# The first batch's attention values loaded in rows of 8 tokens, cast on GpSimd, spread into the key tiles by on-chip DMA, and the output product split in two

## The chip, the cores and the metric

One core of a Trainium2 chip. The metric is the device time of one execution in microseconds (us), median of several; a run is called fast or slow by its state, and ratios use fast runs only. Times inside the kernel are read from profiles of single executions, counted from the start of the span.

## The reference, cut to what matters

```python
# q, k, v: (4 batches, 8 heads, 768 tokens, 64); block = 32, window = 16
k_sum = k.reshape(B, H, 24, 32, D).max(axis=3)
v_sum = v.reshape(B, H, 24, 32, D).mean(axis=3)          # the "means"
scores_l = scale * q @ k^T, kept where |i - j| < 16
scores_s = scale * q @ k_sum^T + log(32)
a = softmax(concat(scores_l, scores_s))
attn = a @ concat(v, v_sum)
x = attn.transpose(0, 2, 1, 3).reshape(3072, 512)
out = ((sigmoid(x @ w_gate)) * (x @ w_val)) @ w_out       # 512 -> 1536 -> 512
```

## The kernel before: the parts that matter

The 768 queries of a batch are cut into 12 query tiles of 64. A query tile needs the 96 tokens around it and the 24 block summaries, so its keys and values are a tile of KX = 96 + 24 = 120 rows. P holds the exponentials of the scores, transposed: 120 rows by 64 queries. The value tile `vx[:, t]` has 96 rows of tokens and 24 rows of means, with ones in column 64 to give the sum of each row. The 24 means are the same for all 12 tiles.

```python
def load_v(b, t0, t1):                       # GpSimd's DMA queue, f32 -> bf16 on the way
    for t in range(t0, t1):
        lo, hi = max(0, QT * t - 16), min(S, QT * t + 80)
        r0 = lo - (QT * t - 16)
        nc.gpsimd.dma_start(out=vx_t[b % 2][r0:r0 + hi - lo, t, :, 0:64],
                            in_=v[b, :, lo:hi, :].transpose([1, 0, 2]))

def V(self, *_):                             # means: 12 matmuls over the 96 rows
    for t in range(NQ):
        nc.tensor.matmul(out=vsp[96:128]..., lhsT=zband[:, 30 - 2 * t:62 - 2 * t],
                         rhs=vx[0:W, t, :, 0:64], start=(t == 0), stop=(t == NQ - 1))
    # ... batch 0: copies to vx[96:120, 0], VectorE spreads to tiles 1-5, a DMA to 6-11

def A(self, p, h=None):                      # output of head pair p (h: half of the queries)
    for t in range(6 * g0, 6 * g1):
        r = 64 * (t % 2)
        for i in range(2):
            nc.tensor.matmul(out=av[r:r + 64, t // 6, (t % 6) // 2, i, 0:65],
                             lhsT=P[0:KX, i, t, :], rhs=vx[0:KX, t, 2 * p + i, 0:65],
                             start=True, stop=True)
    # ... reciprocal and scaling on VectorE

# start of the kernel, batch 0, first half of the queries
for u in a0.units("T2a S1a T3a S2a S3a V A0a A1a X0a A2a X1a"):   # T transposes, S scores,
    u()                                                           # V means, A outputs, X transposes back
f0.m1(0, 0, 0, 1)                            # first feed-forward column block, in slices
a0.A(3, 0)
...                                          # then dense: 24 column blocks, one after the other
```

The weights come by GpSimd's DMA queue, two blocks of columns at a time; the keys and queries of batch 0 and 1 by the queues of SyncE and ScalarE. The profile counts the packets of all of them on the core's 16 DMA engines.

The softmax here doesn't subtract the row's maximum and nothing guards it: scores larger than these inputs give would overflow.

Of the kernel before, what the change touches and what calls it, by code (L numbers as in the profile page):

```python
# [8 lines left out]
FP32 = mybir.dt.float32  # L9
BF16 = mybir.dt.bfloat16  # L10
AX = mybir.AxisListType
ALU = mybir.AluOpType
# [4 lines left out]
def kernel(  # L17
# [10 lines left out]
    nc = tc.nc  # L28

    B, H, S, D = q.shape  # L30
    SCALE = 1.0 / float(D) ** 0.5
    QT = 64
    NQ = S // QT
    W = 96
    NS = S // 32
    KX = W + NS
    NP = H // 2
    d_model = H * D
    d_ff = moe_w_gate.shape[1]
    NF = d_ff // 128  # L40
    HALF = S // 2

    const = ctx.enter_context(tc.tile_pool(name="const", bufs=1))
# [7 lines left out]
    hT_pool = ctx.enter_context(tc.tile_pool(name="hTp", bufs=2))  # L51
# [7 lines left out]
    def ps(shape, dtype, name):  # L59
        return psum.tile(shape, dtype, name=name, tag="mm")  # L60

    def view(ap, off, dims):
        return bass.AP(ap.tensor, ap.offset + off, [list(ap.ap[0])] + [list(d) for d in dims])
# [7 lines left out]
    vx_t = [const.tile([128, NQ, H, 66], BF16, name=f"vx{i}") for i in range(2)]  # L71
    mask = const.tile([128, NQ, QT], BF16, name="mask")
    mask3 = const.tile([W, 3, QT], BF16, name="mask3")
    zband = const.tile([W, 64], BF16, name="zband")

    for t_ in kTn_t:
        nc.vector.memset(t_[:, 0:16], 0.0)
# [9 lines left out]
    def make_masks():  # L87


        nc.gpsimd.memset(mask3, 1.0)  # L90
        nc.gpsimd.affine_select(out=mask3, in_=mask3, compare_op=ALU.is_ge, fill=0.0,
                                base=-1, pattern=[[0, 3], [-1, QT]], channel_multiplier=1)
        nc.gpsimd.affine_select(out=mask3, in_=mask3, compare_op=ALU.is_ge, fill=0.0,
                                base=31, pattern=[[0, 3], [1, QT]], channel_multiplier=-1)
        nc.gpsimd.affine_select(out=mask3[:, 0], in_=mask3[:, 0], compare_op=ALU.is_ge, fill=0.0,
                                base=-16, pattern=[[0, QT]], channel_multiplier=1)
        nc.gpsimd.affine_select(out=mask3[:, 2], in_=mask3[:, 2], compare_op=ALU.is_ge, fill=0.0,
                                base=79, pattern=[[0, QT]], channel_multiplier=-1)
# [7 lines left out]
    def make_zband():  # L106

        nc.gpsimd.memset(zband, 0.0)
        nc.gpsimd.memset(zband[:, 30:32], 1.0 / 32.0)
        nc.gpsimd.affine_select(out=zband[:, 30:32], in_=zband[:, 30:32], compare_op=ALU.is_ge, fill=0.0,  # L110
                                base=-16, pattern=[[-32, 2]], channel_multiplier=1)
        nc.gpsimd.affine_select(out=zband[:, 30:32], in_=zband[:, 30:32], compare_op=ALU.is_ge, fill=0.0,
                                base=47, pattern=[[32, 2]], channel_multiplier=-1)


    def copy(eng, out, in_):
        if eng == "act":
            nc.scalar.copy(out=out, in_=in_)
        elif eng == "dve":
            nc.vector.tensor_copy(out=out, in_=in_)  # L120
        else:
            nc.gpsimd.tensor_copy(out=out, in_=in_)  # L122

    def big():
        return vm_pool.tile([128, 2048], FP32, name="vm", tag="vm")

    def small():
        return nat_pool.tile([128, NP, 6, 128], BF16, name="nat", tag="nat")

    def load_qk(tap, b, p, st, half=None, queue=None):  # L130

        n = S if half is None else HALF
        s0 = 0 if half is None else HALF * half
        T = n // 128
        (queue or nc.sync).dma_start(
            out=st.rearrange("p h t d -> p h (t d)"),
            in_=tap[b, 2 * p:2 * p + 2, s0:s0 + n, :].rearrange("h (p t) d -> p h (t d)", t=T),
        )
        return st

    def staging(T):

        raw = small().rearrange("p a c d -> p (a c d)").bitcast(FP32)
        return [view(raw, 128 * T * i, [[64 * T, 2], [64, T], [1, 64]]) for i in range(12 // T)]
# [16 lines left out]
    def load_v(b, t0, t1):  # L161
# [7 lines that stand above are left out]
    wg_bf = const.tile([128, NP, d_ff], BF16, name="wg")  # L169
    wv_bf = const.tile([128, NP, d_ff], BF16, name="wv")  # L170
    wo_bf = const.tile([128, NF, d_model], BF16, name="wo")

    def load_w(wb, wap, f0, nf):
        nc.gpsimd.dma_start(
            out=wb[:, :, 128 * f0:128 * (f0 + nf)],
            in_=wap.rearrange("(c p) f -> p c f", p=128)[:, :, 128 * f0:128 * (f0 + nf)])
# [9 lines left out]
    class Attention:  # L186
# [61 lines left out]
        def S(self, p, hf):  # L248
# [5 lines left out]
            for t6 in range(6):  # L254
# [12 lines left out]
                    .to_broadcast([128, 2, 6 * QT]),  # L267
                op=ALU.mult)

        def V(self, *_):  # L270
            vx = self.vx
            vsp = ps([128, 512], FP32, "vsp")
            for t in range(NQ):
                nc.tensor.matmul(  # L274
                    out=vsp[96:128].rearrange("p (h d) -> p h d", h=H),
                    lhsT=zband[:, 30 - 2 * t:62 - 2 * t],
                    rhs=vx[0:W, t, :, 0:64],
                    start=(t == 0), stop=(t == NQ - 1))
            src = vsp[96:120].rearrange("p (h d) -> p h d", h=H)
            if self.b == 0:  # L280
                for p in range(NP):
                    copy("dve" if p == 0 else "act", vx[96:120, 0, 2 * p:2 * p + 2, 0:64],
                         src[:, 2 * p:2 * p + 2])
                    copy("dve", vx[96:120, 1:NQ // 2, 2 * p:2 * p + 2, 0:64],
                         vx[96:120, 0:1, 2 * p:2 * p + 2, 0:64]
                         .to_broadcast([NS, NQ // 2 - 1, 2, 64]))
                t0 = NQ // 2
            else:
                nc.scalar.copy(out=vx[96:120, 0, :, 0:64], in_=src)
                t0 = 1  # L290
            self.replicate(t0)


        def L(self, g, h=None):
# [29 lines left out]
        def A(self, p, h=None):  # L324

            P, vx = self.P[p], self.vx
            g0, g1 = (0, 2) if h is None else (h, h + 1)
            G = g1 - g0
            at = psum2.tile([128, 2, 512], FP32, name="av", tag="at")
            av = at[:, :, 0:396].rearrange("p g (a i d) -> p g a i d", a=3, i=2)  # L330
            for t in range(6 * g0, 6 * g1):
                r = 64 * (t % 2)
                for i in range(2):
                    nc.tensor.matmul(  # L334
                        out=av[r:r + 64, t // 6, (t % 6) // 2, i, 0:65],
                        lhsT=P[0:KX, i, t, :],
                        rhs=vx[0:KX, t, 2 * p + i, 0:65],
                        start=True, stop=True)
            avf = at[:, g0:g1, 0:396].rearrange("p g (e d) -> p g e d", d=66)
            rec = xs_pool.tile([128, 2, 6, 1], FP32, name="rec", tag="rec")  # L340
            nc.vector.reciprocal(out=rec[:, 0:G], in_=avf[:, :, :, 64:65])  # L341
            xs = xs_pool.tile([128, 6, 2, 64], BF16, name="xs", tag="xs")
            nc.vector.tensor_tensor(  # L343
                out=xs[:, 0:3 * G].rearrange("p (g a) i d -> p g (a i) d", g=G),
                in0=avf[:, :, :, 0:64],
                in1=rec[:, 0:G].to_broadcast([128, G, 6, 64]),
                op=ALU.mult)
            self.xs[p] = xs
# [72 lines left out]
    def spread(base, extra, lo, hi):  # L421
# [9 lines left out]
        while j < m:  # L431
# [9 lines left out]
    a0 = att[0]  # L441

    raw = [big(), big()]
    sk = [load_qk(k, 0, p, view(raw[p // 2], 768 * (p % 2), [[384, 2], [64, 6], [1, 64]]))
          for p in range(NP)]
    sq = [load_qk(q, 0, p, st, half=0, queue=nc.scalar) for p, st in enumerate(staging(3))]

    def cast0(p):
        srcs[0][p] = [cast_qk(sk[p], "dve"), cast_qk(sq[p], "act")]

    load_v(0, 0, 3)
    make_masks()
    load_v(0, 3, 6)
    make_zband()
    load_v(0, 6, NQ)
    for f0, nf in ((0, 1), (1, 1), (2, 2), (4, 2), (6, 2), (8, 2), (10, 2)):
        for wb, wap in ((wg_bf, moe_w_gate), (wv_bf, moe_w_val)):
            load_w(wb, wap, f0, nf)

    cast0(0)  # L460
    cast0(1)
# [4 lines left out]
    a0.S(0, 0)  # L466
    cast0(3)
    f0 = Ffn(0, xTs[0])
    for u in a0.units("T2a S1a T3a S2a S3a V A0a A1a X0a A2a X1a"):
        u()  # L470
    f0.m1(0, 0, 0, 1)
    a0.A(3, 0)
# [4 lines left out]
    f0.m1(0, 0, 3, 4)  # L477


    for p, st in enumerate(staging(3)):  # L480
        srcs[0][p].append(cast_qk(load_qk(q, 0, p, st, half=1), "pool"))
    for i in range(6):
# [27 lines left out]
    for b in range(B):  # L510
# [7 lines left out]
        else:  # L518
            base = m1[0] + m1[1] + ffn.units2()
# [45 lines left out]
```

## Time and profile before

| | before |
|---|---|
| median time | 255.83 us (255.1 to 258.29, 3 runs) |
| span of the profiled execution | 252.9 us |
| first output product waits until | 22.03 us |
| dense feed-forward work from | 30.99 us |
| first transposes of the second half of the queries | 36.59 us |

(The view of the chain, which the prediction uses, puts the start of a matmul that follows another some 0.2 us later than the timeline does: 31.19 for this 30.99. All starts of dense work below are from the timeline.)

The rows of a timeline are: start, duration, engine, line, operation, output and inputs, shapes, count, and in brackets the idle time before it with what ended it. Two rows of the kernel before: 22 of the 24 output products of head pairs 0 and 1, and the 12 of pair 2. In the chain these twelve take 0.48 us, 0.04 us each.

```profile
22.72 0.61 PE L334 MATMUL av<-vx,P 120*64 120x65 bf16 x22 [0.45 <-DVE vx L120]
24.98 0.55 PE L334 MATMUL av<-vx,P 120*64 120x65 bf16 x12
```

### The profile page before, as it was taken

The page shows a single profiled execution, that of the slowest core. Times are in us where ns is not written, and L with a number is a line of the kernel's source. Part 1 is how long each engine was busy: PE and PEld are TensorE (multiplying, and loading weights), DVE is VectorE, ACT ScalarE, POOL GpSimd, SP SyncE. Part 2 cuts the span into 40 slices and gives each one's busy share as a digit, 9 for nine tenths or more (in the row PEclk, how much of TensorE's full clock was granted, in tenths as well). Part 3 has the DMA queues.
Part 4 walks back from the last instruction along what each step waited for, and adds up shares of the span by engine and source line. Part 5 has one row for each costly group of instructions (what it writes and reads, how often), then busy time and mean ns, then how long its engine had stood idle before and what let it go on. Part 6 is the DMA issues. An engine that isn't in the chain of part 4 may idle for free.

```text
span 252.9 us, 5010 instructions
## 1 busy us (share of the span) xinstructions
PE 232.6 (92%) x1980; PEld 129.6 (51%) x1992; DVE 122.4 (48%) x243; ACT 107.7 (43%) x193; POOL 111.1 (44%) x151
## 2 busy tenths in 40 slices
PE   1666899798999999999999999999999999999993
PEld 1433455466654455555554445555554466665441
DVE  5965237936971331976553307766543034444000
ACT  2851338356874243455551123555511143333121
POOL 8897167389999239996059970000000000000000
PEclk9999579999999999999999999999999999999999
DMA  6999999999999989799999995800024310000132
GB/s 213 241 158 178 221 270 281 268 171 124 128 120 144 212 208 208 148 155 187 194 119 156 223 170 145 126 14 3 0 72 146 116 44 0 1 3 0 49 117 83
DMA packets 100686, 34.25 MB, mean 135 GB/s; under 512 B 84496, under 2 KB 97208, under 8 KB 100280
## 3 DMA queue, kind: packets, MB, share of 16 engines
q0 software_dynamic: 70720, 12.46, 65.0%
q1 hardware_dynamic: 28856, 20.70, 32.5%
q10 hardware_dynamic: 1088, 0.79, 1.0%
q8 instruction: 15, 0.25, 0.4%
q14 instruction: 7, 0.06, 0.1%
HBM read 34.34 MB, written 6.29 MB: 161 GB/s over the span
## 4 chain that ended last, share of the span: by engine, by line
PE 85%; DVE 4%; DMA 2%; ACT 2%; issue 1%; ACTq 0%; DVEq 0%
PE gp L391 26%; PE vp L391 25%; PE m L408 23%; PE sc L257 3%; PE av L334 3%; PE vsp L274 3%; DMA vx<-vx 2%; PE br L362 2%; PE tp L197 1%; DVE vx L120 1%; DVE kTx L233 1%; ACT kTn L203 1%; DVE P L264 1%; DVE kTx L237 0%; DVE xs L343 0%
## 5 line engine op out<-in xcount | busy, mean ns | idle before, releaser
L399 DVE SCALAR_TENSOR_TENSOR hT<-gate,vp 128x384 bf16<-128x384 f32 x96 | 52.8, 551 | 68.7 <-PE vp L391 63.9
L391 PE MATMUL gp<-xT,wg 128*128 128x384 bf16 x384 | 80.6, 332 | 1.1 <-ACT xT L365 1.1
L391 PE MATMUL vp<-xT,wv 128*128 128x384 bf16 x384 | 80.1, 330 | 0.0
L398 ACT ACTIVATE gate<-gp 128x384 f32<-128x384 f32 x96 | 47.3, 493 | 53.6 <-DVE hT L399 43.7
L408 PE MATMUL m<-wo,hT 128*128 128x512 bf16 x276 | 64.3, 379 | 0.6
L391 PEld LDWEIGHTS <-wv 128*128 128x128 bf16 x384 | 37.8, 99 | 26.5 <-issue 2.1
L391 PEld LDWEIGHTS <-wg 128*128 128x128 bf16 x384 | 35.9, 99 | 23.0 <-issue 1.4
L408 PEld LDWEIGHTS <-hT 128*128 128x128 bf16 x288 | 27.0, 98 | 30.7
L166 POOL DMA_DIRECT2D vx<-in_v_dram x48 | 36.8, 798 | 10.5 <-PE sc L257 6.8
L413 ACT ACTIVATE ot<-m 128x512 f32<-128x512 f32 x24 | 14.3, 597 | 52.1 <-PE m L408 51.9
L263 ACT ACTIVATE P<-sc 128x768 bf16<-128x768 f32 x32 | 26.0, 814 | 10.9 <-PE sc L257 10.9
L264 DVE TENSOR_TENSOR P<-P,mask 128x768 bf16<-128x768 bf16 x32 | 20.5, 643 | 13.3 <-ACT P L263 13.3
L305 POOL TENSOR_TENSOR vm<-vm 96x1024 f32<-96x1024 f32 (+4 forms) x20 | 20.5, 1025 | 9.8 <-DMA vm<-in_v_dram 8.4
L343 DVE TENSOR_TENSOR xs<-av,rec 128x768 bf16<-128x768 f32 (+1 forms) x20 | 16.0, 798 | 0.7
L233 DVE TENSOR_REDUCE kTx<-kTn 128x24 bf16<-128x768 bf16 x16 | 15.2, 948 | 2.1 <-ACT kTn L203 2.1
L257 PE MATMUL sc<-qT,kTx 64*128 64x64 bf16 x384 | 12.1, 197 | 4.0 <-DVE kTx L237 2.5
L197 PE MATMUL tp<-ident,qkbf 128*128 128x128 bf16 x96 | 8.9, 253 | 7.0 <-DVE qkbf L120 5.8
L257 PEld LDWEIGHTS <-kTx 64*128 64x128 bf16 x384 | 8.0, 97 | 14.0 <-issue 8.5
L341 DVE RECIPROCAL rec<-av 128x12 f32<-128x12 f32 (+1 forms) x20 | 4.3, 215 | 20.7 <-PE av L334 20.7
L156 POOL DMA_DIRECT2D nat<-in_q_dram x16 | 13.2, 869 | 2.2 <-DMA nat<-in_k_dram 2.2
L122 POOL CAST qkbf<-nat 128x768 bf16<-128x768 f32 (+1 forms) x12 | 8.5, 721 | 12.8 <-DMA nat<-in_q_dram 7.6
L156 POOL DMA_DIRECT2D nat<-in_k_dram x16 | 13.4, 862 | 0.1
(48 smaller groups left out, 111.7 us busy)
## 6 DMA issues: line engine op xcount, KB each, us to landing
out_dram<-ot SPq DMA_DIRECT2D x24, 256.0 KB, 4.3
vx<-in_v_dram POOLq DMA_DIRECT2D x40, 96.0 KB, 5.1
vm<-in_v_dram SPq DMA_DIRECT2D x4, 768.0 KB
vm<-in_k_dram SPq DMA_DIRECT2D x4, 384.0 KB, 6.6
nat<-in_k_dram SPq DMA_DIRECT2D x4, 384.0 KB
nat<-in_q_dram SPq DMA_DIRECT2D x4, 384.0 KB, 13.8
wo<-in_moe_w_out_dram POOLq DMA_DIRECT2D x6, 256.0 KB, 16.2
nat<-in_k_dram POOLq DMA_DIRECT2D x16, 96.0 KB, 4.7
```

Source lines behind the costliest of these rows:

```text
L156: nc.gpsimd.dma_start(out=nat[:, h // 2, :, 64 * (h % 2):64 * (h % 2) + 64], in_=tap[b, h].rearrange("(c p) d -> p c d", p=128))
L166: nc.gpsimd.dma_start(out=vx_t[b % 2][r0:r0 + hi - lo, t, :, 0:64], in_=v[b, :, lo:hi, :].transpose([1, 0, 2]))
L233: nc.vector.tensor_reduce(out=kTx[:, 0, W:KX], in_=kTn[:, 16:16 + S].rearrange("p (n w) -> p n w", w=32), axis=AX.X, op=ALU.max)
L257: nc.tensor.matmul(out=sc[:, i, QT * t6:QT * (t6 + 1)], lhsT=kTx[64 * i:64 * i + 64, t, :], rhs=qT[64 * i:64 * i + 64, QT * t:QT * (t + 1) ...
L263: nc.scalar.activation(out=Ph, in_=sc[:, :, 0:6 * QT], func=ACT.Exp, scale=SCALE)
L264: nc.vector.tensor_tensor(out=Ph, in0=Ph, in1=mask[:, None, 6 * hf:6 * hf + 6, :].rearrange("p i t w -> p i (t w)") .to_broadcast([128, 2, ...
L305: nc.gpsimd.tensor_tensor(out=st[:, 0:n], in0=st[:, 0:n], in1=st[:, n:2 * n], op=ALU.add)
L343: nc.vector.tensor_tensor(out=xs[:, 0:3 * G].rearrange("p (g a) i d -> p g (a i) d", g=G), in0=avf[:, :, :, 0:64], in1=rec[:, 0:G].to_broa ...
L391: nc.tensor.matmul(out=o, lhsT=wb[:, c, 128 * f:128 * (f + 1)], rhs=self.xT[:, c, HALF * hf:HALF * (hf + 1)], start=(c == 0), stop=(c == N ...
L398: nc.scalar.activation(out=gate, in_=gp, func=ACT.Tanh, scale=0.5)
L399: nc.vector.scalar_tensor_tensor(out=self.hT[hf][:, f, :], in0=gate, scalar=1.0, in1=vp, op0=ALU.add, op1=ALU.mult)
L408: nc.tensor.matmul(out=self.m3, lhsT=self.hT[hf][:, f, 128 * tt:128 * (tt + 1)], rhs=wo_bf[:, f], start=(f == 0), stop=(f == NF - 1))
```

## The change

Its intent: batch 0's values came as packets of 128 bytes, and TensorE's means and VectorE's copies then stood in the way of the first output. The new version loads rows of 8 neighbouring tokens (2 KB each), casts them with GpSimd into a buffer that has the ones columns beside them, fills the 96 token rows of each key tile from there by DMA in rows of 1,056 bytes, and takes the means from the same rows in matmuls that fit TensorE's gaps. So that the first outputs need no spread of the means, the output product of the first half is split: 96 token rows from tile t, then 24 rows of means from tile 0, summed in the accumulator.

```diff
+        def Z(self, p, h=None):              # means of one head pair, 8 matmuls
+            for w in range(8):
+                nc.tensor.matmul(out=self.vsp[96:128, 128 * p:128 * p + 128]...,
+                    lhsT=zb, rhs=vb[:, w, 2 * p:2 * p + 2, 0:64], start=(w == 0), stop=(w == 7))
+            if p == NP - 1:
+                nc.scalar.copy(out=self.vx[96:120, 0, :, 0:64], in_=...)
+                self.replicate(1)
 ...                                           # def A
+                    if (self.b, h) == (0, 0):
+                        nc.tensor.matmul(out=o, lhsT=P[0:W, i, t, :], rhs=vx[0:W, t, 2 * p + i, 0:65],
+                                         start=True, stop=False)
+                        nc.tensor.matmul(out=o, lhsT=P[W:KX, i, t, :], rhs=vx[W:KX, 0, 2 * p + i, 0:65],
+                                         start=False, stop=True)
+                        continue
 ...                                           # loads
+    def load_v8(p):
+        nc.sync.dma_start(out=sv[p].rearrange("p (h f) -> p h f", h=2),
+            in_=v[0, 2 * p:2 * p + 2].rearrange("h (p w) d -> p h (w d)", w=8))
+    def cast_v8(p):
+        nc.gpsimd.tensor_copy(out=vb[:, :, 2 * p:2 * p + 2, 0:64], in_=sv[p]...)
+    def place(t, queue):
+        queue.dma_start(out=vx_t[0][r0:r0 + hi - lo, t].rearrange("p h d -> p (h d)"),
+                        in_=vb[lo // 8:hi // 8].rearrange("p w h d -> p w (h d)"))
 ...
-    load_v(0, 0, 3)
     make_masks()
-    load_v(0, 3, 6)
-    make_zband()
-    load_v(0, 6, NQ)
+    make_zb()
+    cast_v8(0)
+    cast_v8(1)
+    load_w(wg_bf, moe_w_gate, 0, 1)
+    cast_v8(2)
+    load_w(wv_bf, moe_w_val, 0, 1)
+    cast_v8(3)
+    for t in range(3):
+        place(t, nc.sync)
+    for t in range(3, 6):
+        place(t, nc.gpsimd)
 ...
-    for u in a0.units("T2a S1a T3a S2a S3a V A0a A1a X0a A2a X1a"):
+    for u in a0.units("T2a S1a Z0 T3a S2a Z1 Z2 Z3 S3a A0a A1a X0a A2a X1a"):
```

More of the change, by code (lines that the diff above doesn't have):

```diff
@@ L74 @@
     zband = const.tile([W, 64], BF16, name="zband")
+    zb = const.tile([W, 32], BF16, name="zb")
     for t_ in kTn_t:
@@ L113, in make_zband, with make_zb @@
                                 base=47, pattern=[[32, 2]], channel_multiplier=-1)
+    def make_zb():
+        nc.gpsimd.memset(zb, 1.0 / 32.0)
+        nc.gpsimd.affine_select(out=zb, in_=zb, compare_op=ALU.is_ge, fill=0.0,
+                                base=0, pattern=[[-4, 32]], channel_multiplier=1)
+        nc.gpsimd.affine_select(out=zb, in_=zb, compare_op=ALU.is_ge, fill=0.0,
+                                base=3, pattern=[[4, 32]], channel_multiplier=-1)
     def copy(eng, out, in_):
@@ L268, in S @@
                 op=ALU.mult)
+        def Z(self, p, h=None):
+            if p == 0:
+                self.vsp = ps([128, 512], FP32, "vsp")
+            for w in range(8):
+                nc.tensor.matmul(
+                    out=self.vsp[96:128, 128 * p:128 * p + 128].rearrange("p (i d) -> p i d", i=2),
+                    lhsT=zb, rhs=vb[:, w, 2 * p:2 * p + 2, 0:64],
+                    start=(w == 0), stop=(w == 7))
+            if p == NP - 1:
+                nc.scalar.copy(out=self.vx[96:120, 0, :, 0:64],
+                               in_=self.vsp[96:120].rearrange("p (h d) -> p h d", h=H))
+                self.replicate(1)
         def V(self, *_):
@@ L279, in V @@
             src = vsp[96:120].rearrange("p (h d) -> p h d", h=H)
-            if self.b == 0:
-                for p in range(NP):
-                    copy("dve" if p == 0 else "act", vx[96:120, 0, 2 * p:2 * p + 2, 0:64],
-                         src[:, 2 * p:2 * p + 2])
-                    copy("dve", vx[96:120, 1:NQ // 2, 2 * p:2 * p + 2, 0:64],
-                         vx[96:120, 0:1, 2 * p:2 * p + 2, 0:64]
-                         .to_broadcast([NS, NQ // 2 - 1, 2, 64]))
-                t0 = NQ // 2
-            else:
-                nc.scalar.copy(out=vx[96:120, 0, :, 0:64], in_=src)
-                t0 = 1
-            self.replicate(t0)
+            nc.scalar.copy(out=vx[96:120, 0, :, 0:64], in_=src)
+            self.replicate(1)
         def L(self, g, h=None):
@@ L333, in A @@
                 for i in range(2):
-                    nc.tensor.matmul(
-                        out=av[r:r + 64, t // 6, (t % 6) // 2, i, 0:65],
-                        lhsT=P[0:KX, i, t, :],
-                        rhs=vx[0:KX, t, 2 * p + i, 0:65],
-                        start=True, stop=True)
+                    o = av[r:r + 64, t // 6, (t % 6) // 2, i, 0:65]
+                    if (self.b, h) == (0, 0):
[4 more added lines that the diff above has]
+                        continue
+                    nc.tensor.matmul(out=o, lhsT=P[0:KX, i, t, :], rhs=vx[0:KX, t, 2 * p + i, 0:65],
+                                     start=True, stop=True)
             avf = at[:, g0:g1, 0:396].rearrange("p g (e d) -> p g e d", d=66)
@@ L443 @@
     raw = [big(), big()]
-    sk = [load_qk(k, 0, p, view(raw[p // 2], 768 * (p % 2), [[384, 2], [64, 6], [1, 64]]))
-          for p in range(NP)]
     sq = [load_qk(q, 0, p, st, half=0, queue=nc.scalar) for p, st in enumerate(staging(3))]
+    held = hT_pool.tile([128, NF, HALF], BF16, name="hT", tag="hT").rearrange("p f n -> p (f n)")
+    held = held.bitcast(FP32)
+    sv = [small().rearrange("p a c d -> p (a c d)").bitcast(FP32)[0:W, 0:1024],
+          small().rearrange("p a c d -> p (a c d)").bitcast(FP32)[0:W, 0:1024],
+          held[0:W, 0:1024], held[0:W, 1024:2048]]
+    vb = hT_pool.tile([128, NF, HALF], BF16, name="hT", tag="hT").rearrange("p f n -> p (f n)")
+    vb = vb[0:W, 0:8 * H * 66].rearrange("p (w h d) -> p w h d", w=8, h=H)
+    nc.vector.memset(vb[:, :, :, 64:66], 1.0)
+    def load_v8(p):
+        nc.sync.dma_start(
+            out=sv[p].rearrange("p (h f) -> p h f", h=2),
+            in_=v[0, 2 * p:2 * p + 2].rearrange("h (p w) d -> p h (w d)", w=8))
+    def cast_v8(p):
+        nc.gpsimd.tensor_copy(out=vb[:, :, 2 * p:2 * p + 2, 0:64],
+                              in_=sv[p].rearrange("p (h w d) -> p w h d", h=2, w=8))
+    def place(t, queue):
+        lo, hi = max(0, QT * t - 16), min(S, QT * t + 80)
+        r0 = lo - (QT * t - 16)
+        queue.dma_start(out=vx_t[0][r0:r0 + hi - lo, t].rearrange("p h d -> p (h d)"),
+                        in_=vb[lo // 8:hi // 8].rearrange("p w h d -> p w (h d)"))
+    sk = []
+    for p in range(NP):
+        sk.append(load_qk(k, 0, p, view(raw[p // 2], 768 * (p % 2), [[384, 2], [64, 6], [1, 64]])))
+        if p > 0:
+            load_v8(p - 1)
+    load_v8(NP - 1)
     def cast0(p):
         srcs[0][p] = [cast_qk(sk[p], "dve"), cast_qk(sq[p], "act")]
-    load_v(0, 0, 3)
     make_masks()
-    load_v(0, 3, 6)
-    make_zband()
-    load_v(0, 6, NQ)
-    for f0, nf in ((0, 1), (1, 1), (2, 2), (4, 2), (6, 2), (8, 2), (10, 2)):
+    make_zb()
[9 more added lines that the diff above has]
+        place(t, nc.gpsimd)
+    for f0, nf in ((1, 1), (2, 2), (4, 2), (6, 2), (8, 2), (10, 2)):
         for wb, wap in ((wg_bf, moe_w_gate), (wv_bf, moe_w_val)):
             load_w(wb, wap, f0, nf)
+    make_zband()
     cast0(0)
@@ L477 @@
     f0.m1(0, 0, 3, 4)
+    for t in range(6, NQ):
+        place(t, nc.sync)
     for p, st in enumerate(staging(3)):
```

## The prediction

> **What bounds the kernel now.** I read the page first, then the chain of waits over the first 60 us, then the timeline of each engine there, then a table by stretches, and last the records of the single DMA packets. From the page I take these lines:
>
> ```profile
> span 252.9 us, 5010 instructions
> PE 232.6 (92%) x1980; PEld 129.6 (51%) x1992; DVE 122.4 (48%) x243; ACT 107.7 (43%) x193; POOL 111.1 (44%) x151
> PE   1666899798999999999999999999999999999993
> PEclk9999579999999999999999999999999999999999
> DMA  6999999999999989799999995800024310000132
> ```
>
> TensorE is full from the sixth slice (32 us) on, with one dip at 45 to 47 us. So the kernel is a start of some 31 us followed by some 220 us of matmuls back to back; the change touches only the start, and whatever it moves the start by moves the end by the same amount, unless something stops TensorE again in between. Two more things are to be seen: the clock is granted at half in slices 5 and 6, and the DMA engines are busy without a pause from 2 us to 60 us.
>
> The chain of waits, in order of time, shows what the start consists of (start us, length us, what):
>
> ```profile
> 16.67 0.45 PE sc L257 x10
> 17.12 4.53 PE vsp L274 x12
> 21.65 0.02 issue
> 21.68 0.31 DVE vx L120
> 21.98 0.02 issue
> 22.01 1.66 DVE vx L120 x4
> 23.67 0.03 issue
> 23.70 0.21 DVE rec L341
> 23.91 0.02 issue
> 23.93 0.57 DVE xs L343
> 24.50 0.05 issue
> 24.55 0.50 PE br L362 x3
> ...
> 31.19 1.28 PE gp L391 x4
> ```
>
> The last scores of the first half end at 17.12; then come the block means (12 matmuls, 4.53 us), a copy, four spreading copies on VectorE (1.66 us), and only then the reciprocal of the first attention output. From 17.12 to 23.70 everything on the chain is the means of the values: 6.58 us. From 24.55 to 31.19 it is outputs, transposes and the first feed-forward column block in slices; from 31.19 it is dense.
>
> The table by stretches (width, busy time and count of PE, PEld, DVE, ACT, POOL, then clock, DMA, GB/s) tells how the transfers do:
>
> ```profile
> 4.00:6.00 2.00, 0.39 (x4) 0.39 (x5) 0.71 (x2) 1.20 (x2) 1.79 (x7) 1.00 1.08 381
> 12.00:14.00 2.00, 1.13 (x11) 1.04 (x11) 1.96 (x5) 1.53 (x3) 2.00 (x3) 1.00 2.42 154
> 20.00:24.00 4.00, 2.50 (x30) 1.13 (x28) 2.23 (x7) 0.59 (x3) 3.75 (x6) 1.00 1.38 175
> 36.00:40.00 4.00, 4.00 (x42) 2.45 (x40) 1.67 (x4) 3.09 (x7) 2.94 (x6) 1.00 1.22 287
> ```
>
> Keys and queries come in at 381 GB/s, the value tiles (128-byte packets) at 154, the weights (512-byte packets) at 175. The packet records give the engine time of one packet when the engines are full: 128 B 13 ns, 256 B 27 ns, 512 B 44 ns, 768 B 42 ns, 1,536 B 64 ns (16 engines over the packets per us). The landings in the trace: value tile 5 at 14.3 us, tile 11 at 18.4; the weights of column blocks 4 and 5 at 27.6, 6 and 7 at 33.0, 8 and 9 at 39.6, 10 and 11 at 46.8.
>
> [...]the 128x512 means matmuls step by 0.427 us[...], and the clock record has 10.24 us[...] at 0.5 from 24.2 to 34.4. [...]from 34 to 36 us GpSimd's queue sent 288 packets of 512 B and SyncE's 270 of 1,536 B. [...]
>
> ```profile
> 40.62 3.13 POOL L122 CAST qkbf<-nat 128x768 bf16<-128x768 f32 x4
> 41.41 2.77 DVE L264 TENSOR_TENSOR P<-P,mask 128x768 bf16<-128x768 bf16 x1 [0.50 <-ACT P L263]
> ```
>
> The mask multiply, 0.56 us when free, took 2.77 us beside four casts back to back.
>
> **The change part by part.**
> Removed: the 12 value DMAs of batch 0, 9,024 packets of 128 B: 9,024 x 13 ns / 16 = 7.3 us of all engines; the means' 4.53 us; the copies' 1.97 us on the chain.
> Added loads: four of 2 heads x 96 rows x 2 KB, 1.57 MB, 4.1 us at 381 GB/s. They sit in SyncE's queue between the key loads. Per engine, from 2.7 us: keys 0 and 1 beside queries (32 pairs x 106 ns) to 6.1; values 0 to 7.6; keys 2 to 9.3; values 1 to 10.5; keys 3 to 11.5; values 2 to 12.5; values 3 to 13.5, or 14.4 if the first weights' packets get in between (1,024 x 27 ns / 16 = 1.7 us for both). Keys 2 now arrive about when VectorE casts them in the kernel before (9.31), keys 3 likewise (11.87): a delay of some 0.3 us.
> Added casts: 96x1024, from the 0.827 us of a 128x768 one, 1.1 us each. GpSimd's order: cast 0 at 7.9, cast 1 at 10.8 to 11.9, a weight issue of 0.8, cast 2 to 13.9, another issue to 14.7, cast 3 to 15.8.
> Added means Z: 8 matmuls of 128 columns cost [...]0.85 us per head pair. Z0 fits the 0.87 us that TensorE waits at 12.0; Z1 to Z3 (2.6 us) have only the 1.79 us gap at 14.5, and Z3 waits for cast 3 (15.8). So the last scores end near 18.0 in place of 17.1.
> Added placing: 96 packets of 1,056 B per tile. SyncE issues tiles 0 to 2 at 15.9, 16.4, 16.9; the shortest SyncE transfers in the trace land 2.0 to 2.5 us after issue: 18.0 to 19.2. GpSimd issues 3 to 5 at 0.8 us each from 15.8; its transfers of about this size take 3.5 to 4 us to land where the engines aren't full: 19.6, 20.4, 21.2. So the first outputs end at 21.3, not 22.7, and the reciprocal, which stood behind the copies to 23.70, starts at 21.4: 2.3 us won.
> Doubled output matmuls: 12 more per head pair at some 40 ns, 0.47 us as the chain has 12. Those of A2 and A3 lie on the chain: 0.9 us given back. Dense work thus starts 1.4 us sooner, 29.8 in place of 31.2.
> The clock: [...]Full clock came 4.0 us after dense work began at 30.4[...].
> Moved: the weights. Before, they had the engines alone from 18.7 to 27, since SyncE's next loads stood behind the means' copy (issue at 22.6, first packet at 27). Now SyncE is through with spreading and placing at about 21.5 and starts the second half of the queries and batch 1's keys and queries some 5 us sooner, while GpSimd starts column block 1 only at 18.2. Sharing packet by packet from 18.5: block 1 (64 packets of each engine) beside the spread and tiles 6 to 11, 71 ns a pair, to 23; blocks 2 and 3 beside the queries, 64 x 86 ns, to 28.9; blocks 4 and 5 beside 1,536 B packets, 64 x 108 ns, to 35.8; blocks 6 and 7 to 42.7; 8 to 11, alone, to 48.4. The same sum for the kernel before, from 27.3, gives 32.8, 39.7 and 46.6 where the trace has 33.0, 39.6 and 46.8, so I trust the arithmetic; not so the start times. The second product of block 6 was wanted at 41.28 before and would be wanted at 40.3: a wait of 2.4 us or so. Against it stands the dip at 45.5 to 47.4 (1.41 us), made by the mask multiplies held up by casts; after such a wait, and with those casts later, it should go.
> Sum: -1.4 start, +0.5 clock, +2.4 weights, -1.4 dip = about 0, where without the weight wait it would be -1 to -3.
>
> **The rivals.** (a) The weights arrive in time, because SyncE's loads start later than I think or the engines lose less to placing: then -1 to -3, if the placed tiles land early even -4, thus 252 to 254.5. For it: weights 8 to 11 had 4 to 6 us of slack. (b) As in the sum, about 255.8. (c) The wait of 2 to 3 us[...]: 257 to 259.5. For it: the window 20.8 to 24.2, half busy, was followed by half clock; against it: the one with the 1.41 us gap was not. (d) GpSimd's four casts hold VectorE's copies on the way to the scores: up to 1.1 us each, [...]up to 1 us more. The reductions (0.95 us, the same beside casts) are immune, and they fill that time.
>
> **Range and chances.** I give (a) 0.45, (b) 0.3, (c) 0.25, since the weights' order looks chosen with care and my start times may be off by 2 us. The middle is then 255.0 us, slightly under the 255.83 of before; 8 in 10 between 251.8 and 259.0. Faster by 2% needs under 250.7, which would take all of the 4.5 us and no wait: 0.06. Slower by 2% needs over 260.9: 0.05. Within 2%: 0.89.
>
> **What would show each step.** The chain between the last scores and the first reciprocal: no means, a landing of the placed tiles, reciprocal at 21.4 (if near 23.7, casts or landings were later than worked out; if near 18.5, placing was cheap). The last scores at 18.0. Dense work from 29.8. A wait of TensorE for weights between 36 and 44, on the product of block 6, is (b); none is (a). A second stretch of half clock after 40 is (c). Mask multiplies or copies of over 0.7 us before 18 us are (d). A time under 251 or over 260 would make the prediction wrong; so would a loss or gain after 60 us, where I expect only a shift.

Three figures in it are my estimates. The 0.85 us of means per head pair is 8 x 0.427 us x 128/512, from the step of the 128x512 means. The +0.5 us for the clock and the 257 to 259.5 us of rival (c) rest on an assumption about how long a half-clock stretch lasts; the trace of before shows one such stretch, of 10.24 us, and no rule for its length.

## The result, and the profile after

| | before | after |
|---|---|---|
| median time, runs of the same rounds | 255.47 us (254.16 to 258.29, 4 runs) | 274.97 us (274.33 to 275.92, 4 runs) |
| span of the profiled execution | 252.9 us | 273.7 us |
| output products run without a further wait from | 22.72 us | 28.63 us |
| dense feed-forward work from | 30.99 us | 50.81 us |
| first transposes of the second half of the queries | 36.59 us | 56.82 us |
| from there to the end of the span | 216.3 us | 216.9 us |

The changed kernel is slower: ratio 1.0785, with a 95% interval of 1.0721 to 1.0848. Here and below a ratio is the mean time of one kernel's fast runs over that of the other's fast runs of the same rounds, so it is not quite the ratio of the medians quoted. The result is correct.

The last two rows of the table are a tool for all that follows. The transposes of the second half of the queries come at the same place of TensorE's program in every variant, 5 to 6 us after dense work begins. I call them the mark. What happens before it is the start; what happens after it shows waits that come later. Here 20.2 of the 20.8 us are lost before the mark.

These lines of the page of the changed kernel answer to those of before: 68 TensorE instructions more, PE's busy time up by 15.9 us (232.6 to 248.5), and slices of 6.8 us that are full from the sixth on, but with other work, as will be seen.

```profile
PE 248.5 (91%) x2048; PEld 141.8 (52%) x2060; DVE 122.3 (45%) x239; ACT 108.0 (39%) x191; POOL 108.7 (40%) x149
PE   1672899898998999999999998999999999999993
```

The chain of waits of the changed kernel (start, length, what), cut:

```profile
7.12 7.76 DMA hT<-in_v_dram
14.94 1.10 POOL hT L478
16.15 0.76 POOL wv L183
16.92 1.05 POOL hT L478
17.99 1.01 SPq L485
...
19.90 8.68 DMA vx<-hT
28.63 0.22 PE av L350
28.84 0.19 PE av L352
...
51.02 1.28 PE gp L409 x4
```

The chain no longer runs through the means. It runs through the third of the four value loads (issued at 7.12, landed at 14.9), two casts with a weight issue between them, the issue of the placing DMAs, and one placing that takes 8.68 us to land; then through output products one by one. L350 is the product over 96 rows, L352 the one over 24 rows, and each takes 0.19 us of the chain where one of before took 0.04 us. The timeline of TensorE shows the three waits for placed tiles:

```profile
19.40 0.50 PE L266 MATMUL sc<-qT,kTx 64*128 64x64 bf16 x12
23.50 0.26 PE L350 MATMUL av<-vx,P 96*64 96x65 bf16 x1 [3.60 <-DMA vx<-hT]
25.99 0.21 PE L350 MATMUL av<-vx,P 96*64 96x65 bf16 x1 [1.66 <-DMA vx<-hT]
28.63 0.22 PE L350 MATMUL av<-vx,P 96*64 96x65 bf16 x1 [1.85 <-DMA vx<-hT]
```

So the 19.8 us by which dense work is late (50.81 - 30.99) fall into two parts. From the last scores to the third tile, TensorE mostly waits: 28.63 in place of 22.72, 5.9 us later. From there to dense work it takes 22.18 us (50.81 - 28.63) in place of 8.27 us (30.99 - 22.72): 13.9 us more, with TensorE busy almost throughout, mostly on these small products. The experiments ask what each part is.

### The profile page after: what moved, and what is told of

Its sections match the earlier page's. It is cut to its first block, busy times and chain, and to the rows that moved or that the text cites. A ratio compares the mean times of both kernels' runs of the same rounds, so it can differ in the third digit from the quotient of the medians.

```text
span 273.7 us, 5161 instructions
## 1 busy us (share of the span) xinstructions
PE 248.5 (91%) x2048; PEld 141.8 (52%) x2060; DVE 122.3 (45%) x239; ACT 108.0 (39%) x191; POOL 108.7 (40%) x149
## 4 chain that ended last, share of the span: by engine, by line
PE 82%; DMA 11%; DVE 2%; POOL 1%; ACT 1%; issue 1%; SPq 1%; ACTq 0%
PE gp L409 24%; PE vp L409 23%; PE m L426 20%; DMA vx<-hT 3%; PE av L350 3%; PE av L352 3%; PE sc L266 3%; DMA hT<-in_v_dram 3%; DMA xT<-xs 3%; PE av L355 2%; DMA nat<-in_q_dram 2%; PE br L380 1%; PE tp L206 1%; PE vsp L297 1%; POOL hT L478 1%
## 5 line engine op out<-in xcount | busy, mean ns | idle before, releaser
L416 ACT ACTIVATE gate<-gp 128x384 f32<-128x384 f32 x96 | 47.3, 492 | 55.5 <-DVE hT L417 43.1
L175 POOL DMA_DIRECT2D vx<-in_v_dram x36 | 27.6, 792 | 12.0 <-PE vp L409 11.1
L273 DVE TENSOR_TENSOR P<-P,mask 128x768 bf16<-128x768 bf16 x32 | 21.8, 684 | 14.1 <-ACT P L272 14.1
L318 POOL TENSOR_TENSOR vm<-vm 96x1024 f32<-96x1024 f32 (+4 forms) x20 | 20.4, 1019 | 17.3 <-DMA vm<-in_v_dram 15.9
L383 ACT COPY xT<-br 128x384 bf16<-128x384 bf16 (+1 forms) x12 | 6.8, 586 | 31.7 <-PE br L380 31.7
L350 PE MATMUL av<-vx,P 96*64 96x65 bf16 x48 | 12.5, 260 | 7.1 <-DMA vx<-hT 7.1
L266 PEld LDWEIGHTS <-kTx 64*128 64x128 bf16 x384 | 8.0, 97 | 13.6 <-issue 8.7
```

The lines of the kernel that those rows point to most:

```text
L266: nc.tensor.matmul(out=sc[:, i, QT * t6:QT * (t6 + 1)], lhsT=kTx[64 * i:64 * i + 64, t, :], rhs=qT[64 * i:64 * i + 64, QT * t:QT * (t + 1) ...
L273: nc.vector.tensor_tensor(out=Ph, in0=Ph, in1=mask[:, None, 6 * hf:6 * hf + 6, :].rearrange("p i t w -> p i (t w)") .to_broadcast([128, 2, ...
L318: nc.gpsimd.tensor_tensor(out=st[:, 0:n], in0=st[:, 0:n], in1=st[:, n:2 * n], op=ALU.add)
L350: nc.tensor.matmul(out=o, lhsT=P[0:W, i, t, :], rhs=vx[0:W, t, 2 * p + i, 0:65], start=True, stop=False)
L416: nc.scalar.activation(out=gate, in_=gp, func=ACT.Tanh, scale=0.5)
```

## The experiments

Twelve kernels ran; the kernel before ran beside each.

**The changed kernel with the product whole again.** VectorE spreads the means to tiles 1 to 5, as before the change.

```diff
-                if (self.b, h) == (0, 0):  # two products, 96 and 24 rows
-                    ...
+                # one product, rows 0:KX, for every half
-                self.replicate(1)
+                nc.vector.tensor_copy(out=self.vx[96:120, 1:6, :, 0:64],
+                                      in_=self.vx[96:120, 0:1, :, 0:64].to_broadcast([NS, 5, H, 64]))
+                self.replicate(6)
```

> The changed kernel with one thing undone: the first-half outputs of batch 0 are again one product over 120 rows (VectorE spreads the means to tiles 1 to 5 first). Both theories of the split [...]expect the outputs back at about 0.04 us each instead of 0.19, the first feed-forward column block dense from about 35.5 us instead of 51.0, and 259 us, plus or minus 2. The placed tiles should still arrive at 23 to 28.6 us. If the placing rather than the split were the main loss, it would stay above 268 us.

Measured: 264.29 us against 254.29 for before (ratio 1.0395, 1.0332 to 1.0458), correct. TensorE's timeline, at the third tile and at two weight waits later:

```profile
28.68 0.77 PE L350 MATMUL av<-vx,P 120*64 120x65 bf16 x20 [2.62 <-DMA vx<-hT]
48.04 0.82 PE L404 MATMUL vp<-xT,wv 128*128 128x384 bf16 x4 [1.85 <-DMA wv<-in_moe_w_val_dram]
55.20 1.20 PE L404 MATMUL vp<-xT,wv 128*128 128x384 bf16 x4 [2.77 <-DMA wv<-in_moe_w_val_dram]
```

The tiles come at the same time as in the changed kernel, but twenty products are done in 0.77 us. Dense work starts at 36.44, 14.4 us sooner than with the split. Of that, only 10.7 us arrive at the end (274.97 - 264.29, the medians), because weights now come too late: 4.6 us of waits at the second products of column blocks 6 and 8, and the granted clock was 0.57 from 55 to 59 us, right after the second wait. The number was higher than expected for that reason: I had left the weights out.

**The kernel before with the split alone**, nothing else of the change.

```diff
-                    nc.tensor.matmul(out=..., lhsT=P[0:KX, i, t, :], rhs=vx[0:KX, t, 2 * p + i, 0:65], ...)
+                    if (self.b, h) == (0, 0):  # the two products of the change, on the kernel before
```

> The kernel before with the split alone: products over 96 and then 24 rows into the same sum, for the first half of batch 0. If the split itself costs (96 products at 0.19 us in place of 48 at 0.04), TensorE loses 16 us in the start: 268 to 272 us. If the 0.19 us came of something else in the changed kernel (late tiles, transfers), 256 to 258 us.

Measured: 267.32 us (ratio 1.052, 1.0468 to 1.0572), correct: the split costs 13 us by itself. TensorE's timeline at the first products:

```profile
22.84 0.26 PE L337 MATMUL av<-vx,P 96*64 96x65 bf16 x1
23.04 0.26 PE L339 MATMUL av<-vx,P 24*64 24x65 bf16 x1
```

Starts are 0.19 to 0.20 us apart. A product's record lasts 0.26 us here and 0.24 to 0.26 us in the second row of before, where neighbours overlap; what is lost is the overlap. Ninety-six such steps are 18.2 us, against 1.9 us for forty-eight of 0.04 us. The difference is 16.3 us; dense work starts 15.2 us later in this kernel's profile (46.20 against 30.99), and 1.4 us come back later because the dip of before at 47.4 us has gone.

**Is it the sum in the accumulator, or the change of rows?** Two more variants of the kernel before. One adds, after each product of the first half, a second one of a zero operand into the same sum, over the same 120 rows. The other adds a product over the 24 rows into columns that nobody reads, so that nothing is summed.

```diff
+# first variant: same rows, accumulating
+                    nc.tensor.matmul(out=o, lhsT=P[0:KX, i, t, :], rhs=zeros[0:KX, 0:65],
+                                     start=False, stop=True)
+# second variant: other rows, not accumulating
+                    nc.tensor.matmul(out=at[r:r + 64, t // 6, 400:465], lhsT=P[W:KX, i, t, :],
+                                     rhs=vx[W:KX, 0, 2 * p + i, 0:65], start=True, stop=True)
```

> The kernel before with a second product into the same sum, but over the same 120 rows (its moving operand is zero, so the result is right). If the cost is the change of row count, the second product costs about 0.04 us: 257 to 258 us. If the cost is the wait for the running sum, it costs 0.15 us and more: 268 to 272 us.

> The kernel before with an extra product over the 24 rows after each product over 120 rows, into unused columns, so nothing is summed. If the cost is the change of row count: 0.19 us for each of the 96 and 268 to 272 us. If it is the wait for the running sum: 0.04 us each and 257 to 258 us.

Measured: the accumulating one 254.78 us (ratio 1.0008, 0.995 to 1.0066; its profiled run was slow and isn't used for times), the one with other rows 267.1 us (1.0531, 1.0459 to 1.0604). Both are correct. Forty-eight further products over the same 120 rows cost nothing that can be told; forty-eight over 24 rows cost 12.8 us. So neither the number of products nor the sum is the cost, but going back and forth between 120 or 96 rows and 24 rows. The three times lie 0.7 to 2.2 us under the ranges expected, too little to change the choice. The timeline of the variant with other rows has the step at two clocks, rows of it:

```profile
24.74 0.21 PE L338 MATMUL av<-vx,P 24*64 24x65 bf16 x1
24.88 0.22 PE L335 MATMUL av<-vx,P 120*64 120x65 bf16 x1
...
25.49 0.26 PE L335 MATMUL av<-vx,P 120*64 120x65 bf16 x1
25.68 0.26 PE L338 MATMUL av<-vx,P 24*64 24x65 bf16 x1
```

Its clock record is full from 22.0 to 25.4 us, where the step is 0.145 us, and half from there on, where it is 0.19 us.

**The changed kernel with the products grouped by rows.** If the alternation is the cost, then twelve products over 96 rows followed by twelve over 24 rows, with the same sums, should be nearly free.

```diff
-            for t in ...: for i in ...:   # 96 rows, 24 rows, 96 rows, 24 rows ...
+            for k0, k1 in ((0, W), (W, KX)):
+                for t in range(6 * g0, 6 * g1):
+                    for i in range(2):    # all over 96 rows, then all over 24 rows
+                        nc.tensor.matmul(out=..., lhsT=P[k0:k1, i, t, :],
+                            rhs=vx[k0:k1, 0 if k0 else t, 2 * p + i, 0:65],
+                            start=(k0, i, t // 2) == (0, 0, 0), stop=(k0, i, t // 2) == (W, 1, 2))
```

> The changed kernel with the same split products in another order: for each pair of heads the twelve over 96 rows first, then the twelve over 24 rows, so the row count changes twice instead of 24 times. [...]an output group takes 24 x 0.04 + 2 x 0.15 = 1.3 us instead of 4.6, dense work starts near 37 us instead of 51, and the time is that of the unsplit version, 264.3 plus or minus 1.5 us, since the weights then bind. If the cost went with the number of products, it would stay near 275.

Measured: 264.08 us against 255.38 (ratio 1.0384, 1.0307 to 1.0461), correct, as expected. All the products of the first two head pairs that were left, 44 of them, in one row of the timeline:

```profile
26.67 1.85 PE L350 MATMUL av<-vx,P 96*64 96x65 bf16 x44 [1.09 <-DMA vx<-hT]
```

Forty-four products in 1.85 us: the doubled count costs about the 0.04 us each that I had assumed. The single records of this trace show both at once: within a group of twelve the starts are 0.03 us apart on average, and from the last of a group to the first of the next, over other rows, it is 0.17 to 0.18 us. Dense work starts at 35.85. The wait for weights is there again, 3.0 us. The split as such is cheap; its order was not.

**Where do the placed tiles lose their time?** Two variants of the grouped kernel read the placing DMA's source from other rows, so their results are wrong (relative error 0.136 and 0.137). In the kernel, a key tile comes from 12 neighbouring partitions. One variant takes 12 rows that are eight partitions apart, the other 96 partitions. They ask whether the placing is slow because its source rows are neighbours, or because there are so few of them.

```diff
-                        in_=vb[lo // 8:hi // 8].rearrange("p w h d -> p w (h d)"))
+                        in_=vb[t % 8:t % 8 + hi - lo - 7:8].rearrange("p w h d -> p w (h d)"))   # 12 rows, 8 apart
+                        in_=vb[0:hi - lo, t % 8].rearrange("p h d -> p (h d)"))                  # 96 partitions
```

> The grouped version with the placed tiles read from 12 rows eight partitions apart instead of 12 neighbouring ones ([...]the result is wrong on purpose). [...]tile 2 is there by 21 to 22 us instead of 28.6 and the outputs start then. If it is slow for [...]its descriptors or the weights beside it, it stays at 26 to 29.

> The grouped version with the placed tiles read from 96 partitions, one row of 1,056 bytes of each ([...]wrong on purpose). [...]tile 2 by 20 to 22 us. [...]if both stay slow, it is the queue or the weights.

Measured: 263.69 us (two runs, ratio 1.0342, 1.0255 to 1.043) and 261.21 us (two runs, 1.0245, 1.0153 to 1.0337); with two runs each, whether they are slower by 2% is unclear. The row of the timeline that the tiles end, in the first and then in the second variant:

```profile
23.87 1.85 PE L350 MATMUL av<-vx,P 96*64 96x65 bf16 x44 [0.16 <-DMA vx<-hT]
```

```profile
23.72 1.85 PE L350 MATMUL av<-vx,P 96*64 96x65 bf16 x44 [0.72 <-DMA vx<-hT]
```

26.67 becomes 23.8, with the last cast ending at 17.4 to 17.6 in all three profiles. But 26.67 is the earliest of the profiles with neighbouring rows: the third tile is used at 28.63 in the changed kernel, at 28.68 with the product whole and at 28.82 in the first variant of the next step, whose placing is the same (last casts at 17.4 to 18.0). So 2.8 to 5 us of the late tiles come from taking all from neighbouring partitions; why these are slower, no run here shows. Whether the transfer had 12 or 96 source partitions made a difference of 0.15 us for the third tile and 0.7 us for the second (23.44 and 22.73). But I had expected the tiles at 20 to 22 us, and they are not. The mark (38.25 and 38.01 in place of 41.89) came 3.6 and 3.9 us sooner; of this 0.4 us (eight apart) and 2.9 us (96 partitions) reached the end, since the weights still made TensorE wait, 2.8 us (96 partitions) and 3.4 us (eight apart), and the granted clock was at half for 6.8 us about these waits in both.

**Can the weights be let past?** The weights share the DMA engines with SyncE's loads of batch 1's keys and queries: from 34 to 36 us of the kernel before, GpSimd's queue sent 288 packets of 512 bytes (weights) and SyncE's 270 of 1,536 bytes (these loads). Three variants hold these loads back by a small DMA in SyncE's queue that depends on a column block of the feed-forward work: the grouped kernel until block 5, the grouped kernel until block 2, and the one with 96 source partitions until block 2.

```diff
+    def batch1_loads():
+        nc.sync.dma_start(out=late_t, in_=f0.hT[0][:, 5, 0:64])      # or block 2
+        for p in range(NP):  # ... the loads and casts of batch 1, as they were
...
+            m1[0][5] = lambda u=m1[0][5]: (u(), batch1_loads())
```

> The grouped version with SyncE's loads of batch 1 held back until the sixth column block is done. If those loads took the weights' turns, the two waits for weights (4.6 us in the unsplit version, and a cold clock behind the second) go: 258.5 to 260.5 us, the 5.2 us over the kernel before that the late tiles cost. If the weights are late for another reason (their late issue alone), it stays at 262 or more.

> The grouped version with batch 1's loads held until the third column block (index 2) is done, some 5 us less than before, so that GpSimd is not late for batch 2 as it was in the last run. If the weights' turns are what the loads take, no wait for weights over 0.5 us is left and the time is 257.5 to 261 us; if it is over 263, the holding back costs as much as the weights' wait, and only the first stage can be compared.

> All three at once: grouped products, placing from 96 partitions (wrong result on purpose), batch 1's loads held until block 2. If the split, the placing and the weights' order are the whole loss, dense work starts at 33 us as in the version that placed from 96 partitions, no wait for weights is left, and the time is 255 to 258.5 us: at best even with the kernel before, since the tiles still arrive 2 to 3 us later than its directly loaded ones are used. Over 261 something else is at work.

Measured: 276.43 us (272.43 to 278.87; two of four runs slow, so no ratio; the two fast ones 272.43 and 275.34), 275.76 us (ratio 1.0775, 1.0698 to 1.0852; its profile slow), and 262.27 us (1.0276, 1.0216 to 1.0336). All three missed. In the first, the waits for weights are gone, and this stands in their place in the view of waits (waiter, releaser, total us, times, longest us):

```profile
PE vp L408 <- DVE hT L416: 11.4, 3, 7.9
```

GpSimd casts batch 1 and issues batch 2's loads in program order, so all of that moved back as well, and TensorE paid for it in waits that end between 110 and 132 us: the chain there runs through GpSimd's work on a later batch (109.9 to 123.2), then a DMA of 5.2 us (kTn<-nat), before TensorE goes on at 131.7. The third kernel kept weight waits of 3.8 us in spite of the hold. Holding transfers back isn't free: what is held must come sometime, and in the page of before the DMA row stays at seven tenths or more up to some 150 us.

**Without the change's machinery: the means spread over the gaps.** The kernel before has the gain within reach in another way. Its 12 means matmuls are split 2, 4 and 6 into TensorE's gaps, and half of the spreading copies go to ScalarE.

```diff
-    ("T2a S1a T3a S2a S3a V A0a A1a X0a A2a X1a")
+    ("T2a S1a V0 T3a S2a V1 S3a V2 A0a A1a X0a A2a X1a")     # 2, 4, 6 means matmuls
-                    copy("dve", vx[96:120, 1:NQ // 2, ...
+                    copy("dve" if p < 2 else "act", vx[96:120, 1:NQ // 2, ...
```

> The kernel before, its value tiles loaded as they were, with the twelve means matmuls of batch 0 put into TensorE's idle gaps (two after the second scores, four after the third, six after the last) and the spreading copies shared between VectorE and ScalarE. Six matmuls of 0.43 us leave the chain, and the first reciprocal no longer stands behind four copies: it starts near 21.2 us instead of 23.7, and the time is 251.5 to 254.5 us[...]. If the tiles bound the means (tile 11 lands at 18.4), 1 us less of it.

Measured: 254.15 us against 255.14 (ratio 0.9967, 0.9922 to 1.0012; six runs), correct: no clear difference. Dense work starts at 27.39, 3.6 us before that of before, and then TensorE's timeline has

```profile
38.24 0.82 PE L396 MATMUL vp<-xT,wv 128*128 128x384 bf16 x4 [0.90 <-DMA wv<-in_moe_w_val_dram]
45.61 0.82 PE L396 MATMUL vp<-xT,wv 128*128 128x384 bf16 x4 [2.89 <-DMA wv<-in_moe_w_val_dram]
```

with a granted clock of 0.50 from 47.0 to 50.3 us. This nearly closes as a sum for the profiled run: -4.1 (the mark, 32.49 against 36.59) + 3.8 (two waits) + 0.5 (a wait for the other weights at 41.9) + 1.7 (half of 3.4 us of half clock) - 1.4 (the dip of before at 47.4, not there) = +0.5, and its span is 253.6 against 252.9.

**The same with part of batch 1's loads held until block 4** (head pairs 2 and 3 only).

```diff
+    batch1_loads(0, 2)                      # at their old place
+            m1[0][4] = lambda u=m1[0][4]: (u(), batch1_rest())   # behind block 4
```

> The early means of the previous call, with the second half of batch 1's loads (head pairs 2 and 3) held back until the fifth column block (index 4) is done. There dense work began at 27.4 us instead of 31.2, and all of it was lost again in waits for the weights of blocks 6 and 8 (4.3 us and a cold clock). If those waits come of taking turns with batch 1's loads, they shrink to under 1.5 us and the time is 250.5 to 253 us, faster than both kernels. If the transfers as a whole are the bound up to 50 us, whatever their order, it stays at 253.5 to 255.5; if GpSimd's casts come too late again, over 256.

Measured: 254.85 us against 254.33 (ratio 1.0018, 0.9964 to 1.0073; six runs), correct. One wait is left, at column block 10:

```profile
48.46 0.82 PE L396 MATMUL vp<-xT,wv 128*128 128x384 bf16 x4 [2.72 <-DMA wv<-in_moe_w_val_dram]
```

So no variant beats the kernel before by a difference that can be told. The mark, with the rest of the span after it, tells why (profiled runs; us):

| kernel | mark | rest |
|---|---|---|
| before | 36.59 | 216.3 |
| after | 56.82 | 216.9 |
| before + split | 52.10 | 214.5 |
| after, product whole | 41.33 | 222.0 |
| after, grouped | 41.89 | 220.0 |
| after, grouped, 96 source partitions | 38.01 | 222.5 |
| before, means in the gaps | 32.49 | 221.1 |
| the same, part of the loads held | 33.28 | 218.8 |

The two of the table that are late by 15 us or more pay hardly anything afterwards (at most 0.6 us). All others in it, before itself apart, pay 2.5 to 6.2 us more after the mark than the kernel before. They are the ones with weight waits. Left out are the variant with other rows (51.23, then 214.2), rows eight apart (38.25, 222.8), the two with a usable profile whose loads are held until block 5 or block 2 (43.44 and 230.0, which paid later as said above; 37.43 and 223.3), and the two whose profiles are slow.

## Why the prediction was wrong

**The step that failed: "Doubled output matmuls: 12 more per head pair at some 40 ns, 0.47 us as the chain has 12. Those of A2 and A3 lie on the chain: 0.9 us given back."** I took the 0.04 us step from products that all have 120 rows and used it for products that alternate between 96 and 24. And I took only A2 and A3 to lie on the chain, where 40 products of A0 and A1 lay on it too, from 28.63 to 36.19. The runs showed a step of 0.19 us for all 96 products, +13 us for the split alone on the kernel before, +12.8 us for the same alternation without a sum, nothing for the same number of products with the same rows, and 1.85 us for 44 once they were grouped. The runs agree with a cost at each change of rows. In the variant with other rows the step is 0.19 us where its clock record is at half and 0.145 us where it is at full; neighbours over equal rows are 0.03 us apart in the grouped kernel. (The clock record of the changed kernel begins only at 55.1 us, and the view by stretches counts what lies before as full: it reads 1.00 from 51 to 55 us while matmuls of 384 columns step by 0.32 us, against 0.16 us from 55.5 on. There the step tells, not the record.) What TensorE does at a change of rows, no run here shows.

**The second: "18.0 to 19.2" for the placed tiles 0 to 2.** They were used at 23.50, 25.99 and 28.63. Three terms of that step were off:

The value loads were to be issued one after the other between the key loads. The timeline of SyncE's queue shows when they were:

```profile
7.12 0.82 SPq L473 DMA_DIRECT2D hT<-in_v_dram  x2
17.99 3.43 SPq L485 DMA_DIRECT2D vx<-hT  x3
```

The last two left at 7.12 and 7.50, the first two at 1.84 and 4.99, though an issue takes half a microsecond (these four took 0.33 to 0.47). The view of waits of SyncE's queue (waiter, releaser, total us, times, longest us) names the landing of query loads, which are in ScalarE's queue and share no buffer with the values:

```profile
SPq L473 <- DMA nat<-in_q_dram: 3.2, 2, 1.9
```

The single records of the trace tell why. A semaphore counts each landing. The first eight loads of the two queues have eight different ones. The ninth, the second value load, waits for the semaphore of the first query load (last counted at 4.97, issue at 4.99), where its own landing is counted as well; the next three loads wait likewise, each for the semaphore that it takes over (the third value load: last count at 7.11, issue at 7.12). So the limit is that this program uses eight semaphores in turn for both queues; nothing in the trace calls for a limit of the queues themselves. No run here used more of them. The third value load landed at 14.9 (worked out: 12.5) and the last at 16.0 (13.5 to 14.4). Since casts 3 and 4 and a weight issue follow one another on GpSimd from 14.94 on, the casts ended at 17.97, not 15.8.

The placings were to take 0.5 us each to issue; three took 3.43 us. They were to land 2.0 to 2.5 us after issue; the last took 8.68 us. The 2.8 to 5 us of neighbouring source partitions are shown. With rows eight apart the third issue still began 1.9 us after the last cast (19.53 against 17.59), and its tile was used 4.3 us later (23.87). Between 18 and 24 us of the changed kernel the packets' times came to 0.88 of the DMA engines' time at 108 GB/s; in the same stretch of before to 1.50, at 175 GB/s (over 1, so the times of packets overlap). So the engines were used less than before there; what held the placings, beyond their neighbouring source rows, isn't shown.

Together with the means gone from the chain, the predicted gain of 1.4 us at the start was a loss of 5.5 us even with the product whole (dense work at 36.44 against 30.99), and of 19.8 us as changed.

**What was right.** Z ran where it was put: Z0 at 12.74, near the gap named, and Z1 to Z3 at 16.72, in one go with the scores before and after them. The means and copies did leave the chain. The last scores ended at 19.9 rather than 18.0. Z didn't wait for the casts there; the scores before it were late, by rival (d) and by the keys. VectorE's cast of keys 3 began at 13.53, not 0.3 but 1.7 us later than before (11.87): these keys landed at 13.4, and beside a GpSimd cast a mask multiply took 1.38 us (0.54 in before, at 11.41, beside no cast), up to 13.6. A copy of 1.06 us (0.22 at 18.21, beside none) beside the next GpSimd cast then made TensorE wait 0.75 us at 16.34. So rival (d) occurred and lay on the way to the last scores, but cost nothing, as the first placed tile came 3.6 us after them. Rival (b), the wait for weights, was right in mechanism and place: in the changed kernel the slow start hid it, and it appeared, at 1.85 to 3.0 us, as soon as the start was repaired, in one variant on the very product named, the second of block 6. The predicted size was 2.4 us. Rival (c), a half-clock stretch after such a wait, followed as well (0.57 and 0.50 in the two profiles quoted). The dip at 47.4 us did go, in the changed kernel and in the variants with weight waits.

The range of 251.8 to 259.0 and the 0.05 for slower failed because all rivals stood on the same mis-sized step: none of them let the split itself be expensive. With the 19.8 us of the start in place of the -1.4, no wait for weights, and its other two terms as they were (+0.5, -1.4), the sum would have been 255.83 + 18.9 = 274.7 us. (The prediction's 9,024 value packets are 8,960 in the trace, which changes its 7.3 us of engine time by less than 0.1.)

**What stays open.** What makes a placing take 4.3 us to land even with its source rows spread; why the last variant's profiled run, 2.1 us ahead at the first transposes of batch 1 (57.25 against 59.35), ends only 0.9 us ahead and has a median with no gain beside it (two later waits of TensorE, 0.5 us at 81 and 0.7 us at 103, are part of the former); and whether some other order of transfers lets the kernel profit from an earlier start. For up to 50 us the transfers are a bound that stands just behind the start: starting 3.6 us sooner gained nothing, as the sum above shows for the profiled run.

## What to carry to other kernels

Keep neighbouring matmuls on the same rows, or group them by rows: an added product costs what the ones around it cost only where it looks like them. Here the step was 0.19 us (0.145 at full clock) with rows alternating and about 0.04 us with the products grouped. Before counting a wait's removal as a gain, ask which bound stands next behind it, here the weights' arrival. An on-chip DMA that spreads a small source may want that source on partitions far apart: here the third tile was used at 23.87 us from rows eight apart, at 26.67 to 28.82 from neighbouring ones. And when an issue waits for a transfer that it shares no data with, look at the semaphores: here two value loads waited 3.2 us for those of query loads.
